# A hand-kept order for 1,876 operations: table instead of list scheduler, with the first loads and zero products rearranged

## The chip, the cores and the metric

One core of a Trainium2 chip runs the kernel. Its engines each work off their own instruction queue, in order: TensorE (PE, with PEld for weight loads), VectorE (DVE), ScalarE (ACT), GpSimd (POOL) and SyncE (SP, which here issues DMAs only; ACT issues some too). The metric is the device time of one execution in microseconds (us); several executions are made and the median is compared. All times below are us unless ns is written, and times "at" a number are counted from the start of the profiled span.

## What is computed

Two layers, each of a linear attention and a gated feed-forward block, on `x` of 2048 rows by 512, with the same weights in both layers:

```python
def _A_ref(x, wqkv, w_phi, wo):          # H = 32 heads of 16
    q, k, v = split(x @ wqkv)
    pq = einsum("bhsd,hdf->bhsf", q, w_phi); pk = einsum("bhsd,hdf->bhsf", k, w_phi)
    phi_q = concatenate([softmax(pq), softmax(-pq)], axis=-1)
    phi_k = concatenate([softmax(pk), softmax(-pk)], axis=-1)
    kv = einsum("bhsf,bhsd->bhfd", phi_k, v); z = einsum("bhsf->bhf", phi_k)
    o = einsum("bhqf,bhfd->bhqd", phi_q, kv) / (einsum("bhqf,bhf->bhq", phi_q, z)[..., None] + 1e-6)
    return o @ wo
def _B_ref(x, W_gate, W_up, W_down):     # 512 -> 1376 -> 512
    gate = x @ W_gate; gate = gate * (gate > 0)
    return (gate * (x @ W_up)) @ W_down
x = x + _A_ref(layernorm(x), ...); x = x + _B_ref(layernorm(x), ...)   # twice
```

## The kernel before

The 2048 rows are 16 tiles of 128 rows; four tiles make a chunk. `X` stays in on-chip memory for the whole run. `setup` issues the first loads: on SP's queue the key half of `wkv`, tile 1, tiles 2-3 and the value half; on ACT's queue tile 0, `w_phi` (`wf`), then, after a first exponential that brings in ACT's table, tiles 4-7, 8-11, the query weights `wq` and tiles 12-15. The remaining weights (`load_weights`, 28 DMAs) go out from SP later.

Each layer runs through these steps, tile by tile:

- **Norm** (`Norm.add`, `normalise`): `bn_stats` and `bn_aggr` on DVE (L388, L390), a few small operations on POOL that make the reciprocal root (L396, L398, L446, L448), then the normalised tile on ACT (L460), DVE or POOL (L472), as a letter of `STEP["xn1"]` says. The tile is transposed by a DMA that SP issues (L486 for two tiles, L490 for one), or by PE with an evacuation on ACT or DVE (L481, letters of `"turn"`).
- **Feature weights** (`feature_weights`): the key half of `wkv` is transposed on PE in four blocks (L351), each evacuated by ACT or DVE (L307, L309, letters of `"wev"`), multiplied with the block-diagonal feature matrix `Wblk` (L364) and evacuated again to `Wk2`. `Wblk` is built on DVE from `wf` (L327). `Wq2` comes later in the same way, with DMA transposes.
- **Keys and values** (`keys_values`, `values`): K product (L710) and V product (L663), four matmuls of 128x512 each; two exponentials on ACT (L715); sums over each head's features on DVE (`feature_sums`: L682 whole, L692 by halves, L688 after POOL has added two halves in L679; a character of `"kr"`: 1 whole, 2 by halves, H one half through POOL, P both); a reciprocal (L724); scaling split between POOL and DVE (L730; the digit of `"ks"` is how many eighths POOL takes); then `L752` adds to the accumulated `kv`.
- **Queries** (`queries`): the same with L794, L798, `"qr"`, L803, a small product on DVE or POOL (L807, `"qq"`), scaling on DVE or POOL (L814, `"qs"`), and a DMA transpose from SP (L816).
- **Attention** (`attention`): product with `R` (L833), division on DVE (L851, L853), transposition by DMA or PE (L866, L873), projection (L884), addition to `X` (L566).
- **Feed-forward** (`glu`, with `Centre`): per chunk, in column parts given by `"part0"`/`"part1"`: gate and up products (L613), evacuations on ACT (L619, L623) and DVE (L626 fused, L630), the rest columns (L593, L598, L600), the down product (L645), and its addition to `X` (L570).

`wake` puts a few products of a zero tile on PE at the very start (L318).

**The order.** Nothing is emitted at once: each step adds an operation to `Plan`, with its engine, an estimated duration, what it reads and writes, and the buffers it holds. `Plan.order` is a list scheduler: it steps through an estimated time and gives each free engine the ready operation with the highest priority, that is, the estimated length of the work that hangs on it plus a bias from `RANK`. `emit` writes the operations in that order, so it is the order of every engine's queue (SP's DMA issues included). Within an engine nothing is overtaken. The same function picks the slot for each buffer: the one that comes free earliest by its estimates. Six 2 KB accumulation buffers (`ps`) are shared by all products of PE.

Of the kernel before, what the change touches and what calls it, by code (L numbers as in the profile page):

```python
# [8 lines left out]
P = 128  # L9
D = 512  # L10
# [3 lines left out]
NDB = D // P  # L14
# [36 lines left out]
TAIL = {"PE": 0.165, "ACT": 0.12, "DVE": 0.115, "POOL": 0.045, "SP": 0.0}  # L51
SAME = {"PE": -0.165, "ACT": 0.035, "DVE": 0.035, "POOL": 0.08, "SP": 0.0}
HOPS = {("DVE", "POOL"): 0.09, ("ACT", "POOL"): 0.15}
NEXT = {"PE": 0.055, "SP": 0.03}
FREE = 0.06


def hop(a, b):
    return SAME[a] if a == b else HOPS.get((a, b), NEXT.get(b, 0.04))


class Plan:
# [10 lines left out]
    def op(self, eng, occ, fn, reads=(), writes=(), holds=(), lat=0.0, at=0.0, group=None, port=False, long=False):  # L73

        o = Op()
        o.eng, o.occ, o.cost, o.fn, o.lat, o.at, o.port, o.long = eng, occ, occ + TAIL[eng], fn, lat, at, port, long
        o.group, o.i_in = group or self.group
        base, slope = RANK.get(f"{o.group}.{eng}") or RANK[o.group]
        o.bias = base - slope * o.i_in
        o.preds, o.succs, o.i = set(), [], len(self.ops)  # L80
# [18 lines left out]
    def order(self):  # L99
        for o in self.ops:  # L100
            for p in o.preds:
                p.succs.append(o)
        for o in reversed(self.ops):
            o.rank = o.cost + o.lat + max([s.rank + hop(o.eng, s.eng) for s in o.succs], default=0.0)
        free = {k: [0.0] * n for k, (pool, n) in self.kinds.items()}
        engines = sorted({o.eng for o in self.ops})
        busy = {e: 0.0 for e in engines}
        ready = {e: [] for e in engines}
        for o in self.ops:
            o.wait, o.t0 = len(o.preds), o.at  # L110
            if not o.wait:
                ready[o.eng].append(o)
        seq, left, now, shut = [], len(self.ops), 0.0, 0.0
        while left:
            moved, later = False, []
            for e in engines:
                if busy[e] > now + 1e-9:
                    later.append(busy[e])
                    continue
                best = None  # L120
                for o in ready[e]:
                    if o.t0 > now + 1e-9:
                        later.append(o.t0)
                        continue
                    if o.port and shut > now + 1e-9:
                        later.append(shut)
                        continue
                    ok = True
                    need = {}
                    for b in o.bufs:  # L130
                        if b.slot is None:
                            need[b.kind] = need.get(b.kind, 0) + 1
                    for k, n in need.items():
                        got = [t for t in free[k] if t is not None]
                        if len(got) < n:
                            ok = False
                        else:
                            t = sorted(got)[n - 1]
                            if t > now + 1e-9:
                                later.append(t)  # L140
                                ok = False
                    if ok and (best is None or (o.rank + o.bias, -o.i) > (best.rank + best.bias, -best.i)):
                        best = o
                if best is None:
                    continue
                o = best
                ready[e].remove(o)
                moved, left = True, left - 1
                o.start, end = now, now + o.cost
                busy[e] = now + o.occ  # L150
                if o.long:
                    shut = end
                later.append(busy[e])
                for b in o.bufs:
                    if b.slot is None:
                        b.slot = min((i for i, t in enumerate(free[b.kind]) if t is not None),
                                     key=lambda i: free[b.kind][i])
                        free[b.kind][b.slot] = None
                        b.end = 0.0
                    b.left -= 1  # L160
                    b.end = max(b.end, end + o.lat + FREE)
                    if not b.left:
                        free[b.kind][b.slot] = b.end
                for s in o.succs:
                    s.wait -= 1
                    s.t0 = max(s.t0, end + o.lat + hop(e, s.eng))
                    if not s.wait:
                        ready[s.eng].append(s)
                seq.append(o)
            if not moved:  # L170
                later = [t for t in later if t > now + 1e-9]
                assert later, "the plan is stuck"
                now = min(later)
        self.seq = seq
        return seq
# [833 lines left out]
```

## Time and profile before

| | |
|---|---|
| time, median of 3 runs | 382.63 (381.41 to 382.69) |
| the profiled execution | 380.91, of which the span is 379.2 |
| PE idle in the span | 379.2 - 363.6 = 15.6 |
| inputs `X` and `wqkv` | 3.5 MB, issued from two queues in the first 5.7 us |
| DMA transposes | 94 of `b`, median 3.2 us from issue to landing; issued by SP one at a time |

The views used are: the page (busy time of each engine); busy time by stretches of the span, where each engine's cell is busy time and number of instructions; the waits of PE; the timeline and the chain of work that ended last, in order of time; and groups of instructions kept apart by shape, where the columns are busy time, mean duration in ns, and idle time before. A PE that is "busy" may still wait inside a pipelined product, so busy PE time is an upper bound of useful time.

### The profile page before, as it was taken

How to read it: one execution, taken by the hardware profiler on the slowest of the kernel's cores; microseconds unless marked ns; L12 is line 12 of the kernel's file. 1: busy time of each engine (PE TensorE's matmuls, PEld its weight loads, DVE VectorE, ACT ScalarE, POOL GpSimd, SP SyncE). 2: the span in 40 equal slices, each digit the busy share in tenths (PEclk: the TensorE clock that was granted, in tenths of full speed). 3: DMA queues.
4: the chain of work that ended last, by engine and by line, in shares of the span. 5: the costliest groups of instructions: out<-in, count | busy, mean ns of one | idle time of the engine just before them, and what ended most of it. 6: DMA issues, size and time to landing. Idle time of an engine off the chain costs nothing.

```text
span 379.2 us, 6724 instructions
## 1 busy us (share of the span) xinstructions
PE 363.6 (96%) x2380; PEld 189.9 (50%) x2409; DVE 268.0 (71%) x608; ACT 205.5 (54%) x439; POOL 121.1 (32%) x203
## 2 busy tenths in 40 slices
PE   4898999999899999999999999999999999999996
PEld 2444545756445444444444456475654445454444
DVE  4999999999925442763497998999962675172433
ACT  4898979776762446737706925865234135514100
POOL 3798965131110220560155681724310002000000
PEclk9999999999999999999999999999999999999999
DMA  8889936788950230021013070478930075000011
GB/s 262 239 143 227 260 44 144 133 149 146 145 107 2 42 58 15 0 30 27 0 22 77 9 119 3 87 127 146 171 85 14 5 146 115 14 0 16 1 55 57
DMA packets 98882, 32.61 MB, mean 86 GB/s; under 512 B 90560, under 2 KB 98336, under 8 KB 98848
## 3 DMA queue, kind: packets, MB, share of 16 engines
q1 hardware_dynamic: 97216, 29.93, 39.7%
q10 hardware_dynamic: 1632, 2.24, 1.8%
q8 instruction: 19, 0.31, 0.4%
q14 instruction: 15, 0.12, 0.1%
HBM read 8.44 MB, written 2.10 MB: 28 GB/s over the span
## 4 chain that ended last, share of the span: by engine, by line
PE 64%; DVE 24%; DMA 6%; issue 2%; ACT 1%; POOL 1%; SPq 0%; POOLq 0%; ACTq 0%
PE ps L613 37%; PE ps L645 14%; PE ps L884 5%; DMA b<-b 4%; DVE sk L682 4%; DVE rk L724 3%; DVE bnst L388 3%; PE ps L794 3%; PE ps L593 3%; DVE sk L692 2%; DVE b L730 2%; PE q L833 2%; DMA X<-in_A_x_dram 2%; DVE sq L682 1%; DVE sk L688 1%
## 5 line engine op out<-in xcount | busy, mean ns | idle before, releaser
L613 PE MATMUL ps<-b,wu 128*128 128x512 bf16 (+2 forms) x400 | 79.2, 336 | 0.6 <-DMA b<-b 0.6
L613 PE MATMUL ps<-b,wg 128*128 128x512 bf16 (+2 forms) x400 | 78.6, 336 | 0.0
L645 PE MATMUL ps<-wd,b 128*128 128x512 bf16 (+3 forms) x368 | 78.1, 366 | 0.3
L623 ACT ACTIVATE b<-ps 128x512 bf16<-128x512 f32 (+2 forms) x100 | 50.5, 520 | 39.6 <-PE ps L613 39.1
L626 DVE SCALAR_TENSOR_TENSOR b<-ps,b 128x512 bf16<-128x512 f32 (+2 forms) x60 | 35.1, 598 | 39.9 <-PE ps L613 38.9
L645 PEld LDWEIGHTS <-b 128*128 128x128 bf16 (+1 forms) x374 | 35.3, 98 | 39.1
L613 PEld LDWEIGHTS <-wg 128*128 128x128 bf16 x400 | 36.1, 98 | 33.1
L613 PEld LDWEIGHTS <-wu 128*128 128x128 bf16 x400 | 36.2, 98 | 32.7 <-issue 0.9
L730 POOL TENSOR_TENSOR b<-b,rk 128x1024 bf16<-128x1024 bf16 (+6 forms) x28 | 37.5, 1351 | 9.6 <-DVE rk L724 7.9
L798 ACT ACTIVATE b<-ps 128x512 bf16<-128x512 f32 x64 | 33.0, 638 | 5.7 <-PE ps L794 5.1
L715 ACT ACTIVATE b<-ps 128x512 bf16<-128x512 f32 x64 | 33.7, 628 | 1.3 <-PE ps L710 1.3
L679 POOL TENSOR_TENSOR b<-b 128x256 f32<-128x256 bf16 x30 | 19.7, 670 | 43.9 <-ACT b L715 34.1
L570 DVE SCALAR_TENSOR_TENSOR X<-ps,r,X 128x512 bf16<-128x512 f32 (+2 forms) x26 | 18.2, 701 | 20.2 <-PE ps L645 20.1
L710 PE MATMUL ps<-Wk,b 128*128 128x512 bf16 x123 | 29.4, 379 | 2.0 <-DMA b<-b 1.2
L884 PE MATMUL ps<-wo,b 128*128 128x512 bf16 x118 | 29.7, 379 | 1.5 <-DMA b<-b 0.9
L630 DVE TENSOR_TENSOR b<-b,b 128x512 bf16<-128x512 bf16 (+2 forms) x40 | 13.5, 348 | 24.0 <-ACT b L623 22.3
L552 POOL TENSOR_SCALAR ve<-tot 128x4 f32<-128x4 f32 x8 | 1.9, 233 | 88.8 <-ACT sq L548 88.8
L663 PE MATMUL ps<-wkv,b 128*128 128x512 bf16 x122 | 29.9, 386 | 0.3
L794 PE MATMUL ps<-Wq,b 128*128 128x512 bf16 x126 | 29.5, 379 | 0.1
L548 ACT ACTIVATE sq<-b 128x512 bf16<-128x512 bf16 x32 | 20.1, 627 | 17.4 <-DVE b L527 17.0
L598 ACT CAST ur<-ps 128x192 bf16<-128x192 f32 (+1 forms) x18 | 5.4, 302 | 32.2 <-PE ps L593 32.1
L814 POOL TENSOR_TENSOR b<-b,rq 128x512 bf16<-128x512 bf16 x19 | 20.2, 1061 | 8.4 <-DVE rq L807 6.1
(94 smaller groups left out, 493.7 us busy)
## 6 DMA issues: line engine op xcount, KB each, us to landing
out_dram<-X SPq DMA_DIRECT2D x15, 128.0 KB, 1.8
X<-in_A_x_dram ACTq DMA_DIRECT2D x3, 512.0 KB, 7.2
b<-b SPq DMA_TRANSPOSE x94, 3.2
wg<-in_B_W_gate_dram SPq DMA_DIRECT2D x8, 160.0 KB, 3.2
wu<-in_B_W_up_dram SPq DMA_DIRECT2D x8, 160.0 KB, 4.0
wd<-in_B_W_down_dram SPq DMA_DIRECT2D x5, 256.0 KB, 4.7
wkv<-in_A_wqkv_dram SPq DMA_DIRECT2D x2, 512.0 KB, 7.1
wq<-in_A_wqkv_dram ACTq DMA_DIRECT2D x1, 512.0 KB, 8.3
```

Source lines behind the costliest of these rows:

```text
L613: nc.tensor.matmul(ps[:], lhsT=wt[:, b, f * P:(f + 1) * P], rhs=xnT[:, lo:hi, b, :], start=(b == 0), stop=(b == NDB - 1))
L623: pl.op("ACT", 0.045 + 0.43 * share, lambda ups=ups, ru=ru, sign=1.0 if fuse else -1.0: nc.scalar.activation(out=ru[:], in_=ups[:], func=A ...
L626: pl.op("DVE", 0.06 + 0.548 * share, lambda gps=gps, ru=ru, h=h, cs=cs: nc.vector.scalar_tensor_tensor(out=h[:, cs], in0=gps[:], scalar=0. ...
L645: nc.tensor.matmul(yps[:], lhsT=hs[f][:fsz, ti * P:(ti + 1) * P], rhs=st.wd[:fsz, f, cols], start=(f == 0), stop=(f == NFT - 1))
L663: nc.tensor.matmul(vp[:], lhsT=xnT[:, ti, kb, :], rhs=st.wkv[:, kb, D:2 * D], start=(kb == 0), stop=(kb == NDB - 1))
L710: nc.tensor.matmul(ps[:], lhsT=xnT[:, ti, kb, :], rhs=w(kb), start=(kb == 0), stop=(kb == NDB - 1))
L715: pl.op("ACT", 0.48, lambda s=s, ek=ek, pk=pk: nc.scalar.activation(out=ek[:, :, s, :], in_=pk[:].rearrange("p (j x) -> p j x", j=8), func ...
L730: eng.tensor_tensor(out=phiK[:, lo:hi, :, :].rearrange("p j s (f h) -> p (j s) f h", h=4), in0=ek[:, lo:hi, :, :].rearrange("p j s (f h) - ...
L794: nc.tensor.matmul(pq[:], lhsT=xnT[:, ti, kb, :], rhs=st.Wq2[:, kb, :], start=(kb == 0), stop=(kb == NDB - 1))
L798: pl.op("ACT", 0.48, lambda s=s, eq=eq, pq=pq: nc.scalar.activation(out=eq[:, :, s, :], in_=pq[:].rearrange("p (j x) -> p j x", j=8), func ...
L814: (nc.vector if on_dve else nc.gpsimd).tensor_tensor(out=e, in0=e, in1=rq[:].unsqueeze(2).to_broadcast([P, 8, DH, 4]), op=Alu.mult)
L884: nc.tensor.matmul(yps[:], lhsT=turned(b), rhs=st.wo[:, b, :], start=(b == 0), stop=(b == NDB - 1))
```

## The change

Four things are changed.

1. `Plan.order` no longer schedules. `ORDER`, a table of 1,876 numbers, lists the operations in the order in which they are emitted; a number is the place at which the program made the operation. Of free slots the one whose last operation stands earliest in the table is taken. `RANK` and the constants of the scheduler are gone; durations given to `op` have no effect any more.
2. The first loads are issued in another order and from other queues (`LOAD_SP`, `LOAD_ACT`); all of ACT's loads now stand ahead of its first exponential.
3. `STEP["wake"]` goes from 3 to 26: 26 zero products, which the table places ahead of and between PE's first operations.
4. The other entries of `STEP` take new values: which engine normalises, evacuates, scales or sums each tile, which tiles are transposed by PE, and in how many parts chunk 0 of the first feed-forward runs.

A second way to make the first keys (`"raw"`) is added but switched off (`"raw": 0`).

```diff
     def order(self):
-        for o in reversed(self.ops):
-            o.rank = o.cost + o.lat + max([s.rank + hop(o.eng, s.eng) for s in o.succs], default=0.0)
...
+        owner = {k: [None] * n for k, (pool, n) in self.kinds.items()}
+        last = {k: [-1] * n for k, (pool, n) in self.kinds.items()}
+        assert sorted(ORDER) == list(range(len(self.ops)))
+        self.seq = [self.ops[i] for i in ORDER]
+        for at, o in enumerate(self.seq):
+            o.place = at
+            assert all(hasattr(p, "place") for p in o.preds), "an operation before what it needs"
+            for b in o.bufs:
+                if b.slot is None:
+                    free = [i for i, u in enumerate(owner[b.kind]) if u is None or not u.left]
+                    b.slot = min(free, key=lambda i: last[b.kind][i])
+                    owner[b.kind][b.slot] = b
+            for b in o.bufs:
+                b.left -= 1
+                last[b.kind][b.slot] = at
+        return self.seq
...
+LOAD_SP = ((0, 1), (1, 2), "f")
+LOAD_ACT = ("k", "v", (2, 4), (4, 8), (8, 12), "q", (12, 16))
...
-    nc.sync.dma_start(out=wkv[:, :, 0:D], in_=wv[:, :, D:2 * D])
-    nc.scalar.dma_start(out=X[:, 0:1, :], in_=xv[:, 0:1, :])
-    nc.scalar.dma_start(out=wf[:], in_=A_w_phi.rearrange("(b j) d f -> (j d) b f", b=NDB, j=8))
-    nc.sync.dma_start(out=X[:, 1:2, :], in_=xv[:, 1:2, :])
-    nc.sync.dma_start(out=X[:, 2:4, :], in_=xv[:, 2:4, :])
-    nc.sync.dma_start(out=wkv[:, :, D:2 * D], in_=wv[:, :, 2 * D:3 * D])
+    parts = {"f": (wf[:], A_w_phi.rearrange("(b j) d f -> (j d) b f", b=NDB, j=8)), "k": (wkv[:, :, 0:D], wv[:, :, D:2 * D]),
+             "v": (wkv[:, :, D:2 * D], wv[:, :, 2 * D:3 * D]), "q": (wq[:], wv[:, :, 0:D])}
+    def load(eng, what):
+        dst, src = parts[what] if isinstance(what, str) else (X[:, what[0]:what[1], :], xv[:, what[0]:what[1], :])
+        eng.dma_start(out=dst, in_=src)
+    for what in LOAD_SP:
+        load(nc.sync, what)
+    for what in LOAD_ACT:
+        load(nc.scalar, what)
...
     nc.scalar.activation(out=wake[:], in_=st.zero[:, 0:1], func=AF.Exp)
-    nc.scalar.dma_start(out=X[:, 4:8, :], in_=xv[:, 4:8, :])
-    nc.scalar.dma_start(out=X[:, 8:12, :], in_=xv[:, 8:12, :])
-    nc.scalar.dma_start(out=wq[:], in_=wv[:, :, 0:D])
-    nc.scalar.dma_start(out=X[:, 12:16, :], in_=xv[:, 12:16, :])
...
-    "part0": "4111", "part1": "6111", "tB0": "D---", "tB1": "--DA", "tA": "----", "wev": "ADADAAAAADDAAAAA",
-    "xn1": "ADAADDAPDAADDAAA", "turn": "A-AA", "wake": 3, "fuse0": "AFAA", "fuse1": "FFFF", "gate": 1, "sA": 2,
-    "xB0": "ADDAAAADAADAADDA", "xB1": "AADDDDADADDADDDD", "xA": "DDDDDDAAADDDAAAA", "xm0": "12221212",
...
+    "raw": 0, "kev": "ADAD", "part0": "3111", "part1": "6111", "tB0": "DD--", "tB1": "-A-A", "tA": "----",
+    "wev": "AADAAAAADDDAAAAA", "xn1": "APADPAADDAADAAAA", "turn": "-A--", "wake": 26, "fuse0": "AFAA",
+    "fuse1": "FAFF", "gate": 2, "sA": 0, "xB0": "AAADAADAADAADDDD", "xB1": "AAAAAAADDADDADDA",
+    "xA": "DDADDDADADDDADAD", "xm0": "11222112", "xmB0": "12221222", "xmB1": "22121122", "xm1": "21121122",
...
-    "ev1": "ADAAADADADAAAADD", "ks0": "7877011827873780", "ks1": "8608218807153351",
-    "kr0": "11H11HH11H2211H1", "kr1": "H22P11H2111222PP", "qr0": "21H1H11P2PH11212", "qr1": "112H121HH1HPP12P",
-    "qs0": "DPPPDDPDPDPPDDPD", "qs1": "PDPPPPDDPDPPDPPP", "qq0": "DPPPDPDPPDPDDPDP", "qq1": "PPPPDDPDPDPPPPDP",
+    "ks0": "7087060677850830", "ks1": "6581334408248588", "kr0": "2HHP11H11PH21HH1", "kr1": "21221HP12P1H212H",
+    "qr0": "12H1H2HPPH2P2H12", "qr1": "21P2111HH22P1P1P", "qs0": "PPPPPPPDDPPDPPPD", "qs1": "DDPPPPPPPPDPPDPP",
+    "qq0": "PPPPPPPPPPDPPPPD", "qq1": "DDDDPPPPPPDDPDPD", "ot0": "ADAADAAAD-AA-A-A", "ot1": "------AA-AAD-ADA",
...
+ORDER = [int(i) for i in """
+0 1 4 142 124 125 139 8 2 3 5 9 10 131 132 141 135 138 145 159 130 11 12 150 160 149 123 151 155 133 15 143 161 6 17
...
+""".split()]
```

Counted off against the numbers, the table gives these queues at the start (tile numbers in brackets, z a zero product). PE: 10 z, first transposition of the key weights, 2 z, two more, and so on, with ten z in all among the parts of `Wk2`; then V[1], 2 z, K[1], z, V[0], z, K[0], z, K[3], V[3], V[2], K[2], z, K[5], K[4]. ACT: normalise tile 0, then seven evacuations of the key weights with that of tile 1 (transposed on PE) among them, then the evacuation of V[1], normalise tiles 2 and 5, exponentials of K[1], evacuation of V[0], exponentials of K[0]. DVE: statistics of tiles 0 and 1, `Wblk` with one evacuation, then the statistics of the other 14 tiles with the normalisations of tiles 3 and 7 between them, then the sums of tile 0. POOL normalises tiles 1 and 4; tiles 0, 2 and 3, which PE transposed before, go through DMA transposes.

More of the change, by code (lines that the diff above doesn't have):

```diff
@@ L47 @@
     pass
[L51 to L59, printed above, removed]
 class Plan:
@@ L113, in order @@
[L113 to L173, printed above, removed]
```

91 lines of the change are left out of this document (43 added, 48 removed), and 96 rows, old and new, of tables (ORDER, RANK, STEP).

## The prediction

> **What bounds the kernel now.** I read the page first.
>
> ```profile
> span 379.2 us, 6724 instructions
> PE 363.6 (96%) x2380; PEld 189.9 (50%) x2409; DVE 268.0 (71%) x608; ACT 205.5 (54%) x439; POOL 121.1 (32%) x203
> PE 64%; DVE 24%; DMA 6%; issue 2%; ACT 1%; POOL 1%; SPq 0%; POOLq 0%; ACTq 0%
> ```
>
> PE is busy for 96% and is idle for 15.6 us. A new order cannot shorten the work of PE, so what it can win lies in those 15.6 us and in products that only wait inside "busy". The third row, the chain of work that ended last, has DVE in 24%: where it is, the stretches tell (busy time by engine).
>
> ```profile
> 0.00:5.00 5.00, 1.46 (x3) 0.29 (x3) 2.00 (x10) 1.49 (x2) 1.32 (x11) 1.00 0.60 156
> 5.00:10.00 5.00, 2.75 (x24) 2.40 (x24) 3.18 (x11) 2.85 (x5) 2.08 (x6) 1.00 1.05 379
> 10.00:15.00 5.00, 4.90 (x24) 2.55 (x26) 5.00 (x16) 3.87 (x7) 3.17 (x10) 1.00 1.00 282
> 15.00:20.00 5.00, 4.54 (x27) 2.23 (x27) 5.00 (x16) 5.00 (x11) 4.64 (x9) 1.00 0.73 175
> 20.00:30.00 10.00, 9.25 (x42) 3.82 (x41) 10.00 (x17) 9.95 (x20) 9.67 (x14) 1.00 0.81 135
> 30.00:40.00 10.00, 9.35 (x91) 5.18 (x92) 10.00 (x20) 8.57 (x17) 8.43 (x11) 1.00 0.97 236
> 40.00:60.00 20.00, 19.12 (x169) 10.27 (x169) 20.00 (x41) 17.24 (x36) 16.21 (x20) 1.00 0.65 153
> 60.00:80.00 20.00, 19.35 (x207) 12.80 (x208) 19.92 (x61) 14.43 (x45) 6.31 (x10) 1.00 0.69 130
> 100.00:120.00 20.00, 18.95 (x100) 9.10 (x100) 10.23 (x24) 11.88 (x29) 2.54 (x4) 1.00 0.46 76
> 220.00:240.00 20.00, 19.68 (x212) 11.46 (x213) 18.26 (x38) 10.23 (x21) 9.37 (x12) 1.00 0.35 52
> 240.00:260.00 20.00, 19.28 (x207) 12.65 (x207) 19.97 (x58) 12.76 (x35) 9.44 (x16) 1.00 0.68 115
> 375.00:380.00 5.00, 1.32 (x23) 1.15 (x21) 1.19 (x3) 0.00 (x0) 0.00 (x0) 0.88 0.18 52
> ```
>
> Idle PE (column 2 less the first) is 5.8 before 10, 2.8 from 10 to 60, 0.65 to 80, 1.05 at 100 to 120, 1.0 at 220 to 260, and 2.9 after 375, where only the last additions and stores are left. From 10 to 60 DVE has no idle time; ACT has none from 15 to 30 and POOL 0.7: the layer's front is bound by these three, by DVE most. The start in order of time:
>
> ```profile
> 1.24 1.46 PE L318 MATMUL ps<-zero 128*128 128x512 bf16 x3 [1.24 <-DVE zero L234]
> ...
> 1.73 1.28 ACT L236 ACT_TABLE_LOAD   x1 [1.73 <-PEq L993]
> ...
> 2.28 0.45 ACTq L238 DMA_DIRECT2D X<-in_A_x_dram  x1
> 3.02 0.20 ACT L236 ACTIVATE wake<-zero 128x1 f32<-128x1 bf16 x1
> 3.85 0.39 ACTq L239 DMA_DIRECT2D wq<-in_A_wqkv_dram  x1
> 3.86 0.69 DVE L388 BATCH_NORM_STATS2 bnst<-X 128x6 f32<-128x512 bf16 x1 [1.09 <-DMA X<-in_A_x_dram]
> ...
> 5.34 0.33 ACTq L240 DMA_DIRECT2D X<-in_A_x_dram  x1
> ...
> 5.37 1.89 PE L351 MATMUL ps<-ident,wkv 128*128 128x128 bf16 x16 [2.66 <-DMA wkv<-in_A_wqkv_dram]
> 6.01 1.07 ACT L307 COPY b<-ps 128x512 bf16<-128x512 bf16 x2 [2.79 <-PE ps L351]
> ...
> 8.21 0.82 ACT L460 ACTIVATE b<-X,ve,rstd 128x512 bf16<-128x512 bf16 x1
> 8.25 0.69 DVE L388 BATCH_NORM_STATS2 bnst<-X 128x6 f32<-128x512 bf16 x1 [0.68 <-DMA X<-in_A_x_dram]
> ...
> 11.65 0.60 ACT L307 CAST Wk<-ps 128x512 bf16<-128x512 f32 x1
> ...
> 12.00 1.80 PE L663 MATMUL ps<-wkv,b 128*128 128x512 bf16 x4
> ```
>
> ```profile
> 15.36 1.03 PE L663 MATMUL ps<-wkv,b 128*128 128x512 bf16 x4
> ```
>
> ```profile
> 19.61 1.10 DVE sk L682
> ...
> 67.97 2.34 PE ps L613 x40
> ...
> 261.37 13.00 PE ps L613 x80
> ```
>
> The last two fences are from PE's own timeline and from the chain. DVE runs without a gap from the statistics of tile 2 at 8.25, and its first sum over features starts at 19.61. `Wk2` is whole at 12.25 (11.65 + 0.60).
>
> **A, the head.** Tile 0 and the key weights change places at the front of the two queues; I keep their times, 3.86 and 5.37. Tiles 2-3 now stand behind the value weights: 1.59 MB lie up to their end (the two halves of the weights 1.05, four tiles of 0.13, and `wf`). 156 GB/s over 5 us bring 0.78 MB, the rest takes 2.1 at 379 GB/s: 7.1 at the earliest, 8.25 as now at the latest; I take 7.6. From there to the first sum DVE now needs 11.36; one copy pair (two of 0.40, which now lie behind 8.25) and one normalisation (0.44, rows below) fall out. DVE alone would begin its sums at 7.6 + 11.36 - 1.24 = 17.7, 1.9 earlier.
>
> ACT has to keep up with that. All seven of its loads now stand ahead of the table. If each issue takes 0.49 (1.79 to 2.28), they are done at 4.2, table and first exponential at 5.7; tile 0's root, there by 8.21 today, I put at 6.2 (statistics end at 4.55, and an estimated 1.6 for the small operations on DVE and POOL); its normalisation (0.82) ends at 7.0, and eight evacuations of 0.59 end at 11.7. But the fifth and sixth issue now came 1.1 late each (2.73 to 3.85, 4.24 to 5.34). Should the last three wait 1.2 each, ACT starts 3.1 later and `Wk2` is whole at 14.8. From there V[1]'s evacuation, two normalisations, K[1]'s exponentials, V[0]'s evacuation and one exponential of K[0] (two of 0.82, and five of some 0.6 like the evacuation at 11.65: 4.7) stand ahead of the first sum: 16.4 or 19.5. So the head wins 1.9 at best, nothing if ACT is held; beyond that it loses. I take -1.2, in between and nearer to DVE, because only two issues of six came late; bounds -1.9 and +1.5 (the third rival says where a loss comes from).
>
> The zero products: three cost 1.46 on a PE that waits anyway. Ten ahead of the key weights take 4.9 at that rate, to 6.1, or less if they become faster on the way; the key weights land at 5.37. Behind them 16 more lie between waits for evacuations; at 0.26 each (1.03 for four) 4.2, of which the last six, among K and V products, may cost 0 to 1.6. In return PE leaves its slow state earlier: four V products took 1.80 at 12.00 and 1.03 at 15.36, 0.77 saved, inside the numbers above.
>
> **B, DVE's work in layer 0.** The durations (busy, mean ns):
>
> ```profile
> L682 DVE TENSOR_REDUCE sk<-b 128x64 f32<-128x1024 bf16 x14 | 16.5, 1197 | 2.7 <-ACT b L715 2.7
> L692 DVE TENSOR_REDUCE sk<-b 128x32 f32<-128x512 bf16 x23 | 14.8, 661 | 0.9 <-ACT b L715 0.9
> L688 DVE TENSOR_REDUCE sk<-b 128x32 f32<-128x256 f32 x13 | 7.4, 575 | 0.2 <-POOL b L679 0.2
> L814 DVE TENSOR_TENSOR b<-b,rq 128x512 bf16<-128x512 bf16 x13 | 5.7, 445 | 0.2 <-POOL rq L807 0.2
> L472 DVE TENSOR_SCALAR b<-X,mv,rstd 128x512 bf16<-128x512 bf16 x9 | 3.8, 436 | 0.7 <-POOL rstd L398 0.7
> L807 DVE TENSOR_TENSOR rq<-sq 128x32 bf16<-128x32 f32 x12 | 2.6, 213 | 0.0
> L679 POOL TENSOR_TENSOR b<-b 128x256 f32<-128x256 bf16 x30 | 19.7, 670 | 43.9 <-ACT b L715 34.1 <-ACT b L798 9.6 <-DVE b L626 0.2
> ```
>
> Sums: "1" is 1.20, "H" 0.66 + 0.58 = 1.24, "P" 1.15, "2" 1.32. Keys go from 9, 5, 0, 2 tiles of these to 6, 6, 2, 2: -0.06. Queries go from 7, 3, 2, 4 to 3, 5, 3, 5: +0.15. Nothing, then, though POOL gets 9 more half-adds of 0.67, 6.0 us. Scaling of queries on DVE falls from 8 tiles to 4: -1.8; L807 from 7 to 2: -1.1; one normalisation beside that in A: -0.4. The eighths of L730 for DVE rise by 9, an estimated 0.11 each (L814 covers as many elements as four): +1.0; one centring and one evacuation more, by the 0.44 of L472: +0.9. Sum -1.4. It counts where DVE binds, from 20 on; bounds 0 (PE has other work meanwhile: it was idle only for 2.8 from 10 to 60) and -2.0.
>
> **C, PE's work.** Chunk 0 of the first feed-forward runs in three parts instead of two: 80 products more. 40 of 128 columns took 2.34 (58.5 ns each), 80 of 384 took 13.00 (162.5): 52 ns per 128 columns and 6.5 fixed, so +0.5. Transpositions on PE: two tiles fewer for the norm, one more each for `tB0` and `ot0`, nothing. For the six zeros I take 0.1. Sum +0.6, bounds 0.5 and 2.1.
>
> **D, the later stalls.** The idle 1.05 at 100 and 1.0 at 220 to 260 stand where DMA transposes and DVE's divisions meet PE's fixed order. All of that order is new. Bounds: -2.1, all gone, and +1.5, waits anew where there are none now. Existing waits can only shrink or move, and most of PE's queue there is feed-forward products that wait for nothing: I take -0.8.
>
> **Sum.** -1.2 - 1.4 + 0.6 - 0.8 = -2.8. The profiled execution of 380.91 (1.7 around its span) becomes 378.1; it lay 1.7 below the median, so in the measure of the runs 382.63 - 2.8 = 379.8. Its own range is 378.0 to 380.7.
>
> **The rivals.** (1) *The whole front moves*: ACT is not held, A -1.9, B -2.0, C +0.5, D -2.1: -5.5, 377.1, and 1 to 2 less if products that now wait inside PE's busy time (1.80 against 1.03 above) go too. For it: DVE has no gap from 10 to 60. Against it: ACT and POOL have hardly more. (2) *No change*: the front is hidden by PE's other work, and only C and D are left: -0.2, 382.4. For it: PE's small idle time there. (3) *ACT is held by its own queue*, slower. If its last issue waits until tiles 2-3 have landed (7.6 in A), its own 0.45, the table and the exponential end at 9.6, and the work that now begins at 6.01 begins 3.6 later. ACT idles for 1.1 from 10 to 15 and not at all from 15 to 30, so at 30 it is 2.5 behind; the 1.4 (30 to 40) and 2.8 (40 to 60) that it has to spare come after the keys that DVE waits for. 382.6 + 2.5 + 0.6 = 385.7. It decides from the point where ACT's first work starts more than 1.1 late, after 7.1. The Trainium skill, page "DMA: Bandwidth & Descriptors" (Issuing engines are not separate DMA queues), says that issuing from several engines only saves the sequencer's issue time; here seven issues are put on one engine with work to do. The rows agree that an issue holds ACT's queue (0.45 at 2.28), and show the longer gaps beside it. (4) *POOL binds*, slower. From 15 to 60 it has 45 - 38.95 = 6.05 to spare, and the 9 half-adds (6.0) take all of it; four scalings and a normalisation come on top. And DVE may stand still beside it:
>
> ```profile
> L814 DVE TENSOR_TENSOR b<-b,rq x13: 355/417/895, 52.1 to 265.8; 128x512 bf16<-128x512 bf16 x13
> ```
>
> The longest is 0.48 over the median. If each of these 14 holds a DVE operation by 0.3, B turns from -1.4 to +2.8, and 382.6 - 1.2 + 2.8 + 0.6 = 384.8. It decides from 5 such, where B is nothing. The Trainium skill, page "SBUF — State Buffer" (Who interferes with whom), states such an exclusive lock of a shared port; by it any DVE operation with two on-chip inputs would stand still for a whole POOL operation. Medians near the shortest (417 and 355) say that it is rare.
>
> **How the numbers follow.** Forecast 0.40, (1) 0.17, (2) 0.16, (3) 0.17, (4) 0.10. A measurement can tell 0.5% from no change, 1.9 us: faster is below 380.7, slower above 384.5. Faster 0.57, same 0.16, slower 0.27. The range takes in (1) and (3), and cuts the far ends of both: 375.8 to 386.0.
>
> **What would show it.** First sum of DVE near 18.4 instead of 19.61; `Wk2` whole by 13; no DVE gap to 55; PE idle from 10 to 60 under 2; DVE durations of L814 and L730 with unchanged medians. The forecast is wrong if ACT's first operation starts after 7.1 and the first sum after 19.6, if POOL is full to 60 with DVE waiting for it, or if PE shows new waits for DMA transposes after 60.

## The result, and the profile after

The changed kernel takes 391.4 us (median of 4 runs, 390.01 to 393.57), the kernel before, run beside it, 382.0 (380.05 to 382.69): a ratio of 1.0254, 95% interval 1.0213 to 1.0295. It is slower by some 9.5 us, outside the predicted range. The profiled execution took 390.01, of which the span is 388.3. In the changed kernel the lines have moved: the key scaling is L676 (before L730), the sums that add to `kv` L698 (L752), the sums over features L612, L618 and L622 (L682, L688, L692), `Wblk` L257 (L327), the product `R` that opens the attention L720 on DVE (L774), the attention's first product L779 (L833).

The page of the changed kernel, its head and busy rows:

```profile
span 388.3 us, 6838 instructions
PE 371.4 (96%) x2475; PEld 198.1 (51%) x2512; DVE 283.6 (73%) x621; ACT 204.2 (53%) x457; POOL 133.0 (34%) x203
```

PE's idle time is 388.3 - 371.4 = 16.9, only 1.3 more than before, but that says little: the 26 zero products count as 10.9 of PE's busy time, against 1.5 of the three before, and most of them fill what was idle time at the start. DVE has 15.6 us more work, though it makes about the same operations (621 against 608). Busy time by stretches of the changed kernel (cells as in the prediction; the number before the last two is the granted clock):

```profile
5.00:10.00 5.00, 2.97 (x18) 1.58 (x16) 1.87 (x7) 3.15 (x5) 3.53 (x5) 1.00 1.06 372
10.00:15.00 5.00, 4.60 (x32) 2.87 (x33) 5.00 (x14) 2.31 (x5) 2.75 (x9) 0.66 0.71 232
...
20.00:30.00 10.00, 9.59 (x49) 4.31 (x49) 8.84 (x21) 10.00 (x20) 8.44 (x19) 1.00 1.04 164
30.00:40.00 10.00, 8.46 (x86) 4.90 (x84) 10.00 (x13) 10.00 (x20) 9.17 (x8) 1.00 0.58 136
40.00:60.00 20.00, 17.57 (x123) 8.58 (x124) 20.00 (x30) 13.38 (x27) 11.58 (x11) 0.91 0.60 175
60.00:80.00 20.00, 17.89 (x180) 11.26 (x184) 19.74 (x47) 14.74 (x39) 16.71 (x25) 0.91 0.48 101
...
100.00:120.00 20.00, 19.17 (x152) 13.00 (x153) 18.52 (x44) 13.78 (x38) 7.03 (x8) 1.00 0.56 105
```

Between 30 and 80 PE is idle for 6.1 (before 2.2), and its clock is down to .91 in two stretches where it was 1.00. DVE is full from 30 to 60 in both kernels, but with fewer instructions in that time: 13 + 30 against 20 + 41. Its instructions became longer.

**The head.** DVE's timeline of the changed kernel, with the tile 2 statistics (the 1.28 at 10.27), the first sum over features, and `R`:

```profile
9.26 0.42 DVE L257 TENSOR_TENSOR Wblk<-M,wf 128x256 bf16<-128x256 bf16 x1 [2.66 <-DMA wf<-in_A_w_phi_dram]
9.60 0.42 DVE L239 COPY b<-ps 128x512 bf16<-128x512 bf16 x1
9.94 0.41 DVE L257 TENSOR_TENSOR Wblk<-M,wf 128x256 bf16<-128x256 bf16 x1
10.27 1.28 DVE L318 BATCH_NORM_STATS2 bnst<-X 128x6 f32<-128x512 bf16 x2
...
20.55 0.65 DVE L622 TENSOR_REDUCE sk<-b 128x32 f32<-128x512 bf16 x1
...
63.80 0.72 DVE L720 TENSOR_TENSOR R<-M,q 128x272 bf16<-128x272 bf16 x2
```

`wf`, now last on SP's queue, comes at 9.2 (before 6.1), and in DVE's order all statistics from tile 2 on stand behind `Wblk`: they start at 10.27 instead of 8.25. The same view of the kernel before has the first sum at 19.53 and `R` at 52.90:

```profile
19.53 1.18 DVE L682 TENSOR_REDUCE sk<-b 128x64 f32<-128x1024 bf16 x1
...
52.90 0.77 DVE L774 TENSOR_TENSOR R<-M,q 128x272 bf16<-128x272 bf16 x2
```

So the head makes DVE's sums 1.0 late (20.55 against 19.53 in this view; the prediction's 19.61 is from the chain), and DVE then idles once for 1.1 (at 25.96), but `R` comes 10.9 late. From `R` to the end of the span the changed kernel takes 324.5, the kernel before 326.3: the whole loss lies ahead of `R`. **The key scaling** is what grew in between. DVE's groups by shape, up to 75 us, of the kernel before and then of the changed one (busy, mean ns):

```profile
L730 DVE TENSOR_TENSOR b<-b,rk 128x128 bf16<-128x128 bf16 x6 | 1.5, 274 | 0.0
...
L730 DVE TENSOR_TENSOR b<-b,rk 128x1024 bf16<-128x1024 bf16 x2 | 1.4, 680 | 0.0
```

```profile
L676 DVE TENSOR_TENSOR b<-b,rk 128x1024 bf16<-128x1024 bf16 x5 | 6.8, 1368 | 0.0
L622 DVE TENSOR_REDUCE sk<-b 128x32 f32<-128x512 bf16 x10 | 6.6, 664 | 0.0
...
L676 DVE TENSOR_TENSOR b<-b,rk 128x128 bf16<-128x128 bf16 x4 | 3.8, 951 | 0.0
```

The same operation takes 1.37 instead of .68 on 1,024 columns and .95 instead of .27 on 128; the sums over features are unchanged (664 ns against 661). All scalings before `R` take 13.4 us against 5.0. Where the time sits is seen beside POOL. DVE's timeline of the changed kernel, then POOL's:

```profile
30.20 2.19 DVE L676 TENSOR_TENSOR b<-b,rk 128x1024 bf16<-128x1024 bf16 x1
...
43.18 4.18 DVE L676 TENSOR_TENSOR b<-b,rk 128x128 bf16<-128x128 bf16 x3
...
54.18 0.61 DVE L676 TENSOR_TENSOR b<-b,rk 128x1024 bf16<-128x1024 bf16 x1
```

```profile
29.93 3.80 POOL L676 TENSOR_TENSOR b<-b,rk 128x1024 bf16<-128x1024 bf16 x2
...
42.80 1.91 POOL L676 TENSOR_TENSOR b<-b,rk 128x1024 bf16<-128x1024 bf16 x1 [1.94 <-DVE rk L670]
44.67 0.67 POOL L609 TENSOR_TENSOR b<-b 128x256 f32<-128x256 bf16 x1
45.29 1.53 POOL L676 TENSOR_TENSOR b<-b,rk 128x768 bf16<-128x768 bf16 x1
...
54.25 1.46 POOL L760 TENSOR_TENSOR b<-b,rq 128x512 bf16<-128x512 bf16 x1
...
63.17 1.05 POOL L760 TENSOR_TENSOR b<-b,rq 128x512 bf16<-128x512 bf16 x1
```

The first of the two POOL scalings in the row at 29.93 runs to about 31.8 (half of 3.80). DVE's starts at 30.20 and ends at 32.39, .6 after it, and .61 is what such a scaling takes when it is not disturbed (the row at 54.18): it stood still until POOL was through. At 43.18 three scalings take 4.18 beside POOL operations that follow one another without a gap. POOL waits in its turn where DVE starts first: its scaling at 54.25, begun during DVE's of 54.18, takes 1.46, and 1.05 at 63.17, where DVE has no such operation. The Trainium skill, page "SBUF — State Buffer" (Who interferes with whom), says just this of a DVE operation with two on-chip inputs beside a GpSimd operation that reads there, and that sums along an axis never contend on this chip; the trace agrees with both.

**PE's fixed order.** PE's waits from 20 to 75 us, and its timeline, of the changed kernel:

```profile
PE q L698 <- DVE b L676: 3.5, 3, 2.0
PE q L698 <- POOL b L676: 2.2, 1, 2.2
```

```profile
44.42 1.03 PE L640 MATMUL ps<-Wk,b 128*128 128x512 bf16 x4
47.42 0.43 PE L698 MATMUL q<-vext,b 128*128 128x68 bf16 x8 [1.97 <-DVE b L676]
47.69 1.54 PE L593 MATMUL ps<-wkv,b 128*128 128x512 bf16 x4
```

PE stands at sums into `kv` whose scaling is late, with value and query products behind them; the four value products at 47.69 then take 1.54 instead of 1.03, at half clock.

### The profile page after: what moved, and what is told of

It is laid out like the page before. It is cut to its first block, busy times and chain, and to the rows that moved or that the text cites. A ratio compares the mean times of both kernels' runs of the same rounds, so it can differ in the third digit from the quotient of the medians.

```text
span 388.3 us, 6838 instructions
## 1 busy us (share of the span) xinstructions
PE 371.4 (96%) x2475; PEld 198.1 (51%) x2512; DVE 283.6 (73%) x621; ACT 204.2 (53%) x457; POOL 133.0 (34%) x203
## 4 chain that ended last, share of the span: by engine, by line
PE 71%; DVE 22%; ACT 2%; DMA 2%; issue 2%; POOL 0%; SPq 0%; DVEq 0%; ACTq 0%
PE ps L543 30%; PE ps L575 18%; PE ps L830 5%; PE ps L593 4%; PE ps L740 4%; PE ps L640 3%; DVE b L676 3%; PE ps L523 2%; DVE sq L622 2%; DVE sk L612 2%; DMA wf<-in_A_w_phi_dram 2%; DVE rk L670 2%; PE q L779 2%; DVE b L560 1%; DVE b L799 1%
## 5 line engine op out<-in xcount | busy, mean ns | idle before, releaser
L543 PE MATMUL ps<-b,wg 128*128 128x512 bf16 (+3 forms) x440 | 81.4, 321 | 0.6 <-DVE X L496 0.6
L553 ACT ACTIVATE b<-ps 128x512 bf16<-128x512 f32 (+3 forms) x110 | 49.9, 488 | 59.1 <-PE ps L543 57.8
L543 PE MATMUL ps<-b,wu 128*128 128x512 bf16 (+3 forms) x440 | 80.3, 321 | 0.5 <-DVE X L500 0.3
L575 PE MATMUL ps<-wd,b 128*128 128x512 bf16 (+4 forms) x363 | 78.8, 366 | 0.6
L676 POOL TENSOR_TENSOR b<-b,rk 128x1024 bf16<-128x1024 bf16 (+7 forms) x26 | 39.2, 1516 | 29.5 <-DVE rk L670 15.7
L556 DVE SCALAR_TENSOR_TENSOR b<-ps,b 128x512 bf16<-128x512 f32 (+2 forms) x50 | 27.3, 574 | 19.9 <-PE ps L543 10.4
L549 ACT ACTIVATE b<-ps 128x512 bf16<-128x512 f32 (+2 forms) x60 | 26.2, 459 | 14.1 <-PE ps L543 13.8
L560 DVE TENSOR_TENSOR b<-b,b 128x512 bf16<-128x512 bf16 (+2 forms) x60 | 22.9, 411 | 13.8 <-ACT b L553 8.0
L496 DVE SCALAR_TENSOR_TENSOR X<-ps,X 128x512 bf16<-128x512 f32 x32 | 21.7, 679 | 6.2 <-PE ps L830 6.2
L454 ACT ACTIVATE b<-X,tot 128x512 bf16<-128x512 bf16 x19 | 13.9, 734 | 20.7 <-DVE X L496 14.4
```

The costliest lines, as they stand in the source:

```text
L543: nc.tensor.matmul(ps[:], lhsT=wt[:, b, f * P:(f + 1) * P], rhs=xnT[:, lo:hi, b, :], start=(b == 0), stop=(b == NDB - 1))
L553: pl.op("ACT", 0.045 + 0.43 * share, lambda ups=ups, ru=ru, sign=1.0 if fuse else -1.0: nc.scalar.activation(out=ru[:], in_=ups[:], func=A ...
L556: pl.op("DVE", 0.06 + 0.548 * share, lambda gps=gps, ru=ru, h=h, cs=cs: nc.vector.scalar_tensor_tensor(out=h[:, cs], in0=gps[:], scalar=0. ...
L560: pl.op("DVE", 0.02 + 0.315 * share, lambda rg=rg, ru=ru, h=h, cs=cs: nc.vector.tensor_tensor(out=h[:, cs], in0=rg[:], in1=ru[:], op=Alu.m ...
L575: nc.tensor.matmul(yps[:], lhsT=hs[f][:fsz, ti * P:(ti + 1) * P], rhs=st.wd[:fsz, f, cols], start=(f == 0), stop=(f == NFT - 1))
L676: eng.tensor_tensor(out=phiK[:, lo:hi, :, :].rearrange("p j s (f h) -> p (j s) f h", h=4), in0=ek[:, lo:hi, :, :].rearrange("p j s (f h) - ...
```

## The experiments

Each run has its ratio to the kernel before, run in the same series; "`R` at" is the start of DVE's L720 (or its line in that kernel) in the profiled execution.

| run | median us | ratio (95%) | `R` at |
|---|---|---|---|
| changed kernel | 391.4 | 1.0254 (1.0213 to 1.0295) | 63.80 |
| e1_wf_first | 387.46 | 1.0129 (1.0106 to 1.0151) | 60.61 |
| e2_old_loads | 387.24 | 1.0123 (1.0083 to 1.0162) | 61.24 |
| e4_before_new_loads | 385.37 | 1.0065 (1.0042 to 1.0088) | 55.80 |
| e6_scale_dve | 391.72 | 1.0236 (1.0209 to 1.0263) | 62.93 |
| e7_sums_later | 388.66 | 1.0181 (1.0147 to 1.0214) | 60.75 |
| e8_no_half | 387.87 | 1.0165 (1.0129 to 1.0200) | 61.23 |
| e9_no_half_later | 389.22 | 1.0202 (1.0170 to 1.0235) | 61.10 |
| e10_before_wf_first | 386.39 | 1.0137 (1.0104 to 1.0171) | 58.01 |
| e11_whole_on_pool | 389.07 | 1.0189 (1.0151 to 1.0226) | 62.67 |
| e12_no_thin | 384.39 | 1.0055 (1.0028 to 1.0081) | 58.27 |
| e13_all_three | 384.33 | 1.0058 (1.0036 to 1.0081) | 58.06 |
| e14_before_no_port_rule | 394.49 | 1.0317 (1.0261 to 1.0372) | 58.19 |
| e15_four | 382.35 | 0.9999 (0.9985 to 1.0013) | 54.83 |
| e16_four_zeros10 | 382.31 | 1.0019 (0.9995 to 1.0043) | 54.70 |
| e17_before_wf_swap | 382.04 | 0.9986 (0.9970 to 1.0001) | 52.91 |
| e18_before_zeros10 | 383.68 | 1.0039 (1.0016 to 1.0061) | 55.13 |
| e19_last_unmoved | 381.21 | 0.9970 (0.9956 to 0.9983) | 54.50 |
| e20_four_wf_last | 386.60 | 1.0125 (1.0104 to 1.0146) | 59.45 |

### The place of the feature weights

e1, in the changed kernel:

```diff
-LOAD_SP = ((0, 1), (1, 2), "f")
-LOAD_ACT = ("k", "v", (2, 4), (4, 8), (8, 12), "q", (12, 16))
+LOAD_SP = ((0, 1), (1, 2))
+LOAD_ACT = ("f", "k", "v", (2, 4), (4, 8), (8, 12), "q", (12, 16))
```

> The changed kernel, with w_phi moved from the third place of SP's queue to the first of ACT's; nothing else. Theory H (the head): w_phi lands at 9.2, DVE waits 2.7 for it with tile 2 long there, and the fixed order runs out of step, from which the long scalings on DVE, PE's waits of 2.0 and 2.2 for them and the slow clock follow: w_phi lands by 5.5, first statistics of tile 2 by 8.0 instead of 10.27, time 383 to 386. Theory P (the order itself makes DVE's scalings meet POOL's, whatever the head does): only the 2.3 at the head move, and part is lost again: 389 to 391, with DVE scalings of 1024 columns still over 1.0 in the mean.

e2, the changed kernel with all first loads as before (order and queues), and e4, the kernel before with the changed kernel's first loads and nothing else:

> The changed kernel with the first loads of the kernel before (queues, sequence and place); table and engine choices stay. H: w_phi at 6.0 again, but value weights at 12 and tiles 2-3 at 8.2: 384 to 387. P: 389 to 392.

> The kernel before with the changed kernel's first loads and nothing else of it. H and P alike: DVE's queue has w_phi's product ahead of the statistics of tiles 1 and 2, so DVE waits to 9.2 and its front moves by 2 to 3.5: 384 to 386. If the time stays within 1 of 382, late w_phi is not what costs.

With the weights first, `Wblk` no longer waits in e1 and the first sum comes at 18.30:

```profile
5.46 0.43 DVE L257 TENSOR_TENSOR Wblk<-M,wf 128x256 bf16<-128x256 bf16 x1
...
18.30 0.65 DVE L622 TENSOR_REDUCE sk<-b 128x32 f32<-128x512 bf16 x1
```

The ratio falls from 1.0254 to 1.0129: 4.8 us of 382. e2 wins as much. Both end between the ranges of the two theories (e2 just above the first), so each theory has a part. e4 shows the loss without the new order: `Wblk` waits 4.44 for `wf`, until 9.24, and the kernel before becomes 2.5 us slower; e4 moves all the first loads, so this is not the price of `wf` alone. The other half of the loss is not the loads: in e1 and e2 `R` is still 8 us later than before, and e1's scalings of 1,024 columns still take 1.40 on average. A later run, e20, puts `wf` back on SP's queue after every repair below (e15): it comes at 11.0, later still than in the changed kernel, `R` 4.6 later, and by the ratios the time is 4.8 us longer.

> The kernel with all four repairs (382.35 us) with the feature weights put back where the change has them, last on SyncE's queue. If late weights cost by themselves, whatever the order behind, tile 2's statistics start near 10.2 us again and the time is 385 to 387 us. If the order's slack hides them once the port is free, within 1 us of 382.4.

Late weights cost 4.8 us in the changed kernel and 4.8 once it is repaired. Why 16 KB come so late is in the DMA view of the changed kernel from 5 to 9 us (packets, MB, share of the time of 16 engines; q1 is SP's queue):

```profile
q10 hardware_dynamic: 812, 1.47, 99.2%
q1 hardware_dynamic: 531, 0.02, 7.6%
```

`wf` is 512 runs of 32 bytes (128 rows by 4 blocks by 16 numbers), and they are SP's packets here: while q10 moved 812 packets of 1.8 KB on average, q1 moved 531 packets with 0.02 MB in all. The Trainium skill, page "DMA: Bandwidth & Descriptors" (Queues, rings and completion order), says that an engine takes packets from its queues in turn; the two counts, near one another while the sizes are far apart, agree. That is the second part of the delay. In the first, from the issue at 1.71 to 5.9, SP's queue moved tiles 0 and 1, which stand ahead of `wf` on it (288 packets with 0.26 MB, beside 907 of q10). Ahead of all other loads on the other queue (e1) `wf` took 2.7 from issue to landing instead of 7.5.

### DVE's scaling beside POOL

e14 is the test from the other side: the kernel before, without three lines of its scheduler. An operation marked `port` (the scalings with two inputs) was never planned to start while a `long` one of POOL runs.

```diff
-                    if o.port and shut > now + 1e-9:
-                        later.append(shut)
-                        continue
```

> The kernel before, its scheduler without the three lines by which VectorE starts no two-input operation while a long one of GpSimd runs; loads, zero products and all costs as before. If that rule is what kept the scaling off the port, its 12 scalings before R take 8 to 13 us instead of 5.0, R comes 3 to 8 us later than 52.9, and the time is 385 to 391 us. If the port does not decide: scaling under 6 us, 381 to 384 us.

Groups of DVE by shape, up to 75 us, of e14:

```profile
L727 DVE TENSOR_TENSOR b<-b,rk 128x128 bf16<-128x128 bf16 x6 | 4.9, 817 | 0.0
...
L727 DVE TENSOR_TENSOR b<-b,rk 128x1024 bf16<-128x1024 bf16 x2 | 2.4, 1198 | 0.0
```

The planner orders anew without the rule; the same 12 scalings as before now take 11.2 instead of 5.0, and `R` comes 5.3 later, both as expected. The time is 12 us longer, above the range and more than `R` says. The rule also kept the second layer: over the whole run the key scalings on DVE take 20.3 instead of 10.2, and the second layer's `R` comes 10.7 later (243.72 against 233.05). This is the changed kernel's fault made alone: durations of .27 and .68 are what that rule bought, and with the scheduler it left.

e6, in the changed kernel, gives POOL's part of the key scaling of layer 0 to DVE:

```diff
-            pl.op("POOL", 0.14 + 0.2165 * cut, lambda scale=scale, cut=cut: scale(nc.gpsimd, 0, cut), reads=deps,
+            by = "POOL" if L == "1" else "DVE"
+            pl.op(by, 0.14 + 0.2165 * cut, lambda scale=scale, cut=cut, e=nc.gpsimd if L == "1" else nc.vector: scale(e, 0, cut), reads=deps,
```

> The changed kernel, but POOL's part of the key scaling in layer 0 (72 eighths) is issued on DVE at the same places of the table. It costs DVE some 5.4. P: without long POOL operations beside them DVE's scalings of 1024 columns come back from 1.37 to 0.7, 7.3 saved in all, and PE's 2.2 wait for POOL goes: 387 to 390. H: the front is late anyway and DVE gets more work: 393 to 397.

DVE's scalings of e6, up to 75 us:

```profile
L676 DVE TENSOR_TENSOR b<-b,rk 128x1024 bf16<-128x1024 bf16 x8 | 5.4, 690 | 0.0
...
L676 DVE TENSOR_TENSOR b<-b,rk 128x128 bf16<-128x128 bf16 x4 | 1.3, 327 | 0.0
```

The durations are healed, the time is not, and it lies between the two ranges: 24 scalings take 14.0 on DVE where 13 took 13.4. POOL's share saved DVE .6 us in all; the rest of its help went into the standstill.

Three runs on top of e1 take work off the meeting of DVE and POOL instead. e8 leaves POOL's 21 half-additions of layer 0 to DVE, e11 gives tiles 1, 4, 6 and 12 whole to POOL, e12 gives POOL the thin last eighth of tiles 0, 3, 8 and 9 (the table keeps its order; numbers of operations that fall away are taken out). In this order, with the changed entries of `STEP` alone:

```diff
-"kr0": "2HHP11H11PH21HH1", "qr0": "12H1H2HPPH2P2H12"
+"kr0": "2222112112221221", "qr0": "1221222222222212"
...
-"ks0": "7087060677850830"
+"ks0": "7887868677858830"
...
-"ks0": "7087060677850830"
+"ks0": "8088060688850830"
```

> The changed kernel with the feature weights first on ScalarE's queue, and layer 0 without its 21 half-additions on GpSimd: VectorE makes these sums itself, in two instructions as for the letter 2. If GpSimd's many instructions hold VectorE's scaling at the shared port, the 1,024-column scaling falls from 1.39 us to under 1.0 on average, and VectorE gains more than the 2.6 us (21 times .55 less .425) that the longer sums cost it: 383.5 to 386 us. If the order's waits decide and not the port: 387 to 389 us, with TensorE's waits at the key-value sums at 5 us or more.

> The changed kernel with the feature weights first (387.5 us), and of the key scaling of layer 0 the whole tiles 1, 4, 6 and 12 on GpSimd instead of VectorE, at the same place of the table. VectorE has worked without a gap from 20 us, and makes R at 60.5 us against 52.9 us in the kernel before: its 13 scalings before R took 13.6 us against 5.0. If the time held at the port is what the order costs, four scalings of 1.37 us leave VectorE, R comes at 55 to 57 us, and the time is 383 to 385.5 us. If the order's waits on other engines decide, GpSimd's 2 us for each make them later: R past 59 us and 387 us or more.

> The changed kernel with the feature weights first, and the 128-column piece of VectorE in the key scaling of tiles 0, 3, 8 and 9 given to GpSimd, which scales the other 896 columns of these tiles. By work the four pieces are 4 times .22 = .9 us; by the port they cost VectorE 4 times .95 = 3.8 us, since they meet GpSimd's own piece of the same tile. Port: R at 56.5 to 58 us, 384 to 386 us. Work alone: R at 59.5 us, 386.5 to 388 us.

e12 alone wins, 2.8 us by the ratios, and `R` comes 2.3 earlier: the four pieces had cost DVE 3.8 (4 of .95) where undisturbed ones take 1.1 (4 of .27). e8 brings the 1,024-column scalings down to .95 as expected, but the 128-column ones rise to 1.06 beside POOL's own scalings, and DVE has the longer sums to pay: nothing is left, and the time is that of e1 within the intervals. e11's second range came true: DVE's scalings fall to 10.4, but PE now waits for POOL:

```profile
PE q L698 <- POOL b L676: 6.3, 2, 5.0
```

### PE's fixed order

e7 moves each group of `kv` sums of layer 0 in the table of e1 behind the next three other products of PE (22 of 24 could be moved); e9 is e8 with that.

> The changed kernel with the feature weights first on ScalarE's queue (387.5 us), and in the table TensorE's groups of key-value sums of layer 0 moved later, each behind the next three other products; nothing else moves. If the 6.6 us that TensorE stands still at these sums between 30 and 62 us are head-of-line waits (what is ready stands behind what is not), they fall under 2 us, no window of half clock is left after 15 us, and the time is 382 to 384.5 us. If what is late is VectorE itself, held at the port, the sums are only waited for at another place (recorded values, first query products, banks): 386.5 to 388.5 us.

> Both: no half-additions of layer 0 on GpSimd, and the key-value sums of layer 0 three products later. If port and fixed order each have a part, 381 to 383.5 us, under both runs beside it; if it is the order alone, as the run with the sums moved (within 1 us); if neither, 387 us.

Neither won anything: e7 lies at the top of its second range, and e9 is no faster than e7 or e8. In e7 the waits for DVE fall to 1.0, but a wait of 3.7 for POOL and 1.0 for `R` appear, and `R` is no earlier (60.75): with DVE as late as before, PE only runs out of work later. e13 puts the repairs of e8, e11 and e12 together:

```diff
-"kr0": "2HHP11H11PH21HH1", "qr0": "12H1H2HPPH2P2H12", "ks0": "7087060677850830"
+"kr0": "2222112112221221", "qr0": "1221222222222212", "ks0": "8888868688858830"
```

> The feature weights first, no half-additions of layer 0 on GpSimd (which makes room there), the 128-column pieces of tiles 0, 3, 8, 9 and the whole tiles 1, 4, 6, 12 on GpSimd. If VectorE up to R is the bound and the port is what loads it, R comes at 51 to 54 us and the time is 379.5 to 383 us, at or under the kernel before. If it stays over 385 us, R is not what the end hangs on.

DVE's scalings up to `R` are down to 4.7, and yet `R` comes at 58.06. (Only five of the 13 are left on DVE, and they are not undisturbed: by the durations of e6 and of the kernel before they would take 2.2. The one of 640 columns takes 2.20 instead of .48.) PE's and then DVE's timeline of e13 have the reason:

```profile
37.92 0.62 PE L698 MATMUL q<-vext,b 128*128 128x68 bf16 x14 [3.21 <-POOL b L676]
```

```profile
44.24 1.22 DVE L612 TENSOR_REDUCE sk<-b 128x64 f32<-128x1024 bf16 x1 [3.98 <-ACT b L661]
```

PE stands at sums that need POOL, the key products behind them come late, so do their exponentials on ACT, and DVE, with less to do, idles for 4.0. e15 is e13 with the sums four products later; e19 moves them by three, and leaves those of tiles 12 to 15, for which `R` waits, where the change has them.

> Feature weights first, no half-additions on GpSimd in layer 0, the scalings of tiles 0, 1, 3, 4, 6, 8, 9, 12 whole on GpSimd (together 384.3 us), and now the key-value sums of layer 0 four products later in TensorE's order as well. Without the last, VectorE's scalings before R took 4.7 us and R still came at 58.1 us: TensorE stood 3.2 us at sums that waited for GpSimd, the next key product came late, and VectorE waited 4.0 us for its exponentials. If that chain is what is left, the two waits are gone, R comes at 53 to 55.5 us, and the time is 379.5 to 382 us. If the sums only wait elsewhere, as they did when they alone were moved: 384 to 386 us.

> The kernel with all four repairs, but the key-value sums are moved by three products only, and those of tiles 12 to 15, which R waits for, stay at the change's place. In the run with all moved by four, VectorE waited .77 us for the last sums ahead of R. If R is what the end of the front hangs on, it comes near 54 us instead of 54.8 and the time is 381 to 382 us, at or just under the kernel before. If moving them was what kept TensorE busy, 382.5 to 384 us.

In e15 both waits are gone, `R` comes at 54.83, and the kernel is level with the one before (0.9999). `R` had waited .77 for the last sums:

```profile
54.83 0.79 DVE L720 TENSOR_TENSOR R<-M,q 128x272 bf16<-128x272 bf16 x2 [0.77 <-PE q L698]
```

In e19 that wait is gone, and it is the fastest, 381.21, by 0.3% (0.2 to 0.4) under the kernel before: the changed kernel with its weights first, eight of its 13 scalings before `R` taken from DVE, and its sums later. It differs from e15 in two things, three products instead of four and the last tiles left in place, which were not told apart. Whether e8's and e11's edits are needed beside e12's once the sums are moved was not tried.

### Zero products, and smaller things

e16 is e15 with the first 10 zero products alone, e18 the kernel before with 10 instead of 3, e17 the kernel before with `wf` and tile 0 exchanged on ACT's queue, e10 the kernel before with e1's loads, 10 zeros, and its planner's arrival times set to those loads. The edits of e18, e17 and e10:

```diff
-"wake": 3
+"wake": 10
...
-    nc.scalar.dma_start(out=X[:, 0:1, :], in_=xv[:, 0:1, :])
     nc.scalar.dma_start(out=wf[:], in_=A_w_phi.rearrange("(b j) d f -> (j d) b f", b=NDB, j=8))
+    nc.scalar.dma_start(out=X[:, 0:1, :], in_=xv[:, 0:1, :])
...
-WF_IN, WK_IN, WV_IN, WQ_IN, LOADED = 3.4, 4.2, 6.7, 10.4, 11.0
+WF_IN, WK_IN, WV_IN, WQ_IN, LOADED = 4.0, 5.7, 7.2, 12.1, 11.5
...
```

> The same with the first 10 of the 26 zero products alone. If the 16 later ones lie only where TensorE would be idle, within 0.5 us of the run beside it; if they stand in front of work, up to 1.5 us faster; if they hold the clock up, a window of half clock in the first 20 us and 1 to 2 us slower.

> The kernel before with 10 zero products instead of 3, placed by its own scheduler. If seven more zeros cost nothing, as TensorE has nothing to do before the keys land at 5.4 us, within 0.5 us of 382; if they hold the ring's banks or run on into the transposes at half clock, up to 1 us slower.

> The kernel before with one swap: the feature weights' load ahead of X's tile 0 on ScalarE's queue. VectorE's wait of 1.3 us for the weights at 6.1 us shrinks, tile 0 comes about .45 us later. If the weights are on the path of the old order too, 380.5 to 381.8 us; if keys or X's tiles 2 and 3 end last there, no change within 0.5 us.

> The kernel before with its scheduler, with the changed kernel's first loads but the feature weights first on ScalarE's queue, ten zero products, and the planner's arrival times set to these loads. If late feature weights are the whole cost of the new loads (385.4 us with them last), this is back at or under the kernel before: 379.5 to 382.5 us. If the loads of the values and keys ahead of X's later tiles cost by themselves, 383.5 to 386 us.

The 16 later zeros make no difference that can be told (e16). In the kernel before seven more make it 0.4% slower; its first sum comes at 21.76 instead of 19.53, and the clock is down to .57 from 12 to 16 us, so more zeros did not keep it up. Its scheduler orders the rest around them (DVE now waits 1.58 for POOL at 21.34), so the cost is that of zeros and order together. e17 shows no difference: `wf` comes earlier, tile 0 later (its statistics at 5.81 instead of 3.86), and the first sum stays (19.41). e10 is inconclusive: its planner, given the new times, put ACT's second normalisation at 16.79 and DVE waited 3.47 for its first exponentials, so loads and order can't be told apart; its time lies above both of its ranges.

## Why the prediction was wrong

**What bounds** was read rightly: DVE sets the front, and over the changed kernel and its repairs the time follows `R`, from end to end about one for one (63.8 to 54.5 against 391.4 to 381.2), though not run by run (e7 has the `R` of e1 and is .5% slower).

**B, the step that failed.** "Scaling of queries on DVE falls ...", "The eighths of L730 for DVE rise by 9, an estimated 0.11 each", sum -1.4: it kept the durations of the kernel before. With the undisturbed durations of e6 and of the kernel before the changed kernel's 13 scalings would take 6.0 (5 of .68, 4 of .27, 2 of .28, .49 and .48), +1.0 against 5.0 as reckoned; they took 13.4, so 7.4 were standstill. The prediction had the mechanism as rival (4), with a chance of .10 and .3 for each meeting, and dismissed it with "Medians near the shortest (417 and 355) say that it is rare." It was rare because a rule of the old scheduler kept the two apart, and that rule is among the lines which the diff removes; e14 shows it by taking the three lines out alone. The sign of the rival was right; the price per meeting was up to 1.6 (2.19 less .61).

**A, the second failure.** -1.2 with a first sum near 18.4 instead of 19.61; it was 20.55, against 19.53 in the same view. With `wf` first it is 18.30 (e1), so X, the key weights and ACT were costed well enough. What was never priced is `wf`, moved last on SP's queue, with DVE's statistics queued behind `Wblk`. That costs 4.8 (changed kernel to e1) and 4.8 (e15 to e20); in the old order the new loads together cost 2.5 (e4).

**Rival (3)**, ACT held: the sign named for it came, ACT's first work at 7.41 (after 7.1) and the first sum at 20.55 (after 19.6). But in e1 ACT starts at 6.96 and in e2 at 6.22, and their times agree within .3 us: it is not what decides. `Wk2` is whole at 15.87, not by 13, since its products wait for `Wblk`; ACT itself idles 2.64 for PE at 11.81.

**The zeros**: the 16 later ones cost nothing that can be told, inside the 0 to 1.6 given. PE did leave its slow state earlier, as forecast: the record of its granted clock has full speed from 7.10, in the kernel before from 13.57 (where its stretches show 1.00 before that, nothing is on record). But it fell back to half from 10.51 to 13.92, after PE's wait of 2.43 for `Wblk`. **C** was not run by itself.

**D, the later stalls**, "can only shrink or move": PE's idle time at 100 to 120 went from 1.05 to .83, which agrees in sign, and what lies behind `R` (C, D and a part of B) takes 1.8 less. But new waits came earlier, 5.7 at L698, each the other side of a fixed order: where an input is late, what is ready stands behind it. Two windows of half clock followed them. By the repairs' ratios the account is: late weights 4.8 (1.0254 to 1.0129), work taken off the meeting of DVE and POOL 2.7 (to 1.0058, e13; e12's edit alone, 1.0055, wins as much), the place of the sums 2.3 (to .9999, e15) and 1.1 (to .9970, e19). The last two causes are intertwined, so their shares hold for this order of repairs alone: the sums moved alone won nothing (e7), and without it DVE, with less to do, was left waiting (e13).

## What to carry to other kernels

A duration read from a trace belongs to the order under which it was taken: before keeping it, look whether the code that is removed kept two engines apart (here one rule of the scheduler, worth 12 us). A small load is priced by what the other queue moves beside it, and by what stands behind its first reader in that engine's order. In a fixed order a group that waits for a slower engine belongs a few products behind ready work, but only once the slower engine itself is less held (e7 against e15).

## What was not expected of the hardware

PE's waits of 1.97 and 2.17 were each followed by a stretch at half clock. Busy time by stretches of the changed kernel:

```profile
48.00:50.00 2.00, 2.00 (x7) 0.71 (x6) 2.00 (x4) 0.68 (x2) 0.39 (x1) 0.51 0.99 349
...
62.00:64.00 2.00, 1.91 (x26) 1.47 (x25) 1.97 (x5) 0.00 (x0) 1.92 (x3) 0.50 0.04 8
```

The Trainium skill, page "TensorE: Matmul & The Clock Gate" (Part 1), ties the half clock to an idle window of about 3.4 us that runs freely; here a gap of 2 us was enough. And 16 KB in runs of 32 bytes took 7.5 us behind two tiles of its own queue and beside the other queue's large loads, where the same load took 2.7 ahead of them.
